# A fused sliding-window attention and two-layer MLP: weight loads in a row, a mask product on another engine, wider unused matmuls, and later steps placed anew

## The chip, the cores and the metric

The kernel runs on one core of a Trainium2 chip. The core has five engines that run their own instruction streams side by side: TensorE (PE in the profile, its weight loads PEld), VectorE (DVE), ScalarE (ACT), GpSimd (POOL) and SyncE (SP), which here only issues DMAs. The metric is device time in microseconds (us) of one execution.

## The reference

Input are q, k, v of shape (8 batches, 8 heads, 576 positions, 64), and two weight matrices, 512 x 2048 and 2048 x 512, all float32.

```
scores = (1/sqrt(64)) * q @ k^T                 # per batch and head, 576 x 576
scores = where(|i - j| <= 32, scores, -1e9)     # a band of 65 positions
attn   = exp(scores - max) / (sum + 1e-9)
x      = (attn @ v), heads side by side         # 4608 tokens x 512
h      = x @ w_in                               # 4608 x 2048
g      = max(0.01 * h, h)
out    = g @ w_out                              # 4608 x 512
```

## The kernel before

The schedule is written out by hand: what stands first in the program stands first on its engine, and each engine works strictly in that order.

**Attention.** The work is cut into steps i of a batch, a half of its 576 positions (288) and a pair of heads; i = 0 to 7 is batch 0 (first the four pairs of the first half), 8 to 15 batch 1. For each step `score(i)` (lines 411 to 439) multiplies the K blocks with Q on TensorE into one PSUM tile `ps`, ScalarE takes the exponential, and one engine multiplies the result with a 0/1 mask: VectorE where `masked_by=nc.vector` is given, GpSimd otherwise (line 436). `sums(i)` multiplies the masked result with a block matrix of ones on TensorE (`row_sums`, line 461) and takes the reciprocal on VectorE (`inverse`, line 469). `product(i)` multiplies it with V (line 484), and `scaled(i)` multiplies product and reciprocal on VectorE into `xT` (line 503). The PSUM tiles `x` (products) and `s` (row sums) have one buffer each; the row sums of steps 1 and 2 lie in the ring of four buffers `mm` that the MLP's first layer uses too. Masks are made on GpSimd and VectorE at the start.

**Loads of batches 0 and 1.** `load_qk(b, p)` (lines 68 to 97) issues one DMA for Q and one for K of a pair on SyncE. With `behind` given, a 1x1 memset on an engine (line 75) comes first, so that SyncE's issues start only when that engine has got there. `cast_qk` (line 280) casts what landed to bf16 on VectorE or GpSimd, and `transposes(b)` turns it on TensorE (line 322 for batch 0, 326 for batch 1), with copies on ScalarE. `load_cast_v` (line 147), `load_w_in` (line 687) and `load_w_out` (line 691) are DMAs that cast on the way; GpSimd issues them, so each stands in GpSimd's own order between its masks and casts. W_in comes in four loads of 512 columns, W_out in four loads of 512 rows.

**The MLP.** `h_first(0)` does the first four tiles (f = 0 to 3) of the first layer, column block by column block, as xT becomes ready; `h_tile(0, f)` does the other twelve, four matmuls of 288 columns each (line 527). Between them `second_half()` takes the next step of batch 0's second half: product, scaling, the row sums of the following step, and a score. After that come the first layer for the second half, `second_pair(p)` (transposes and casts of batch 1's pairs; the K casts of pairs 0 to 3 stand on GpSimd), and the second layer (lines 597 and 613). From then on a plan made at build time puts the attention of the other batches between the matmuls.

**Unused matmuls.** `warm_up(n, w)` (lines 622 to 628) issues n matmuls of 128 columns whose result nobody reads, at four places of the start: 28, 6, 8 and 4. The first 28 take a zeroed piece of the sixth `prob` buffer (`idle`, line 160), the others `ones_bd`.

Of the kernel before, what the change touches and what calls it, by code (L numbers as in the profile page):

```python
# [16 lines left out]
def kernel(  # L17
# [15 lines left out]
    nc = tc.nc  # L33
# [7 lines left out]
    NPAIR = H // 2  # L41
# [26 lines left out]
    def load_qk(b, p, behind=None):  # L68

        for into, src, name in ((qf, q, "qf"), (kf, k, "kf")):
            t = fload.tile([128, 2 * RUN * D], FP32, name=f"{name}{p}")
            if behind is not None:
                behind.memset(t[0:1, 0:1], 0.0)
                behind = None
            heads = src[b, 2 * p:2 * p + 2]
            if b == 0:

                into[b, p] = t[:, 0:NB * D]  # L80
                nc.sync.dma_start(
                    out=into[b, p], in_=heads.rearrange("a (p c) d -> (a p) (c d)", c=NB))
                continue
            t = t[0:96].rearrange("p (a r) -> p a r", a=2)
            if b < BY_DMA:
                nc.sync.dma_start(out=t, in_=heads.rearrange("a (p c) d -> p a (c d)", c=RUN))
            elif into is qf:
                nc.sync.dma_start(
                    out=t.rearrange("p a (g e) -> p a g e", g=3),
                    in_=heads.rearrange("a (g p c) d -> p a g (c d)", g=3, c=2),  # L90
                )
            else:
                nc.sync.dma_start(
                    out=t.rearrange("p a (c d) -> p a c d", d=D),
                    in_=heads.rearrange("a (c p) d -> p a c d", p=96),
                )
            into[b, p] = t
# [45 lines left out]
    def load_cast_v(b, p, heads=range(2)):  # L143

        for a in heads:
            r = slice(64 * a, 64 * a + 64)
            nc.gpsimd.dma_start(  # L147
                out=vbd[b % 2][r, p, :, r],
                in_=v[b, 2 * p + a].rearrange("(c p) d -> p c d", p=64),
            )  # L150

    NPROB = 6
    prob = const.tile([128, NPROB, 2, HALF], BF16)
# [3 lines left out]
    zero = const.tile([128, 1], BF16)  # L157
    nc.vector.memset(zero, 0.0)

    idle = prob[:, NPROB - 1, 0, 0:128]  # L160
    nc.vector.memset(idle, 0.0)
    for p in range(2):
        nc.vector.memset(vbd[0][:, p], 0.0)
# [3 lines left out]
    ones_bd = const.tile([128, 128], BF16)  # L167
# [18 lines left out]
    for lo in (0, 64):  # L186
        w = win[lo:lo + 64]
# [170 lines left out]
    def where(i):  # L358
        return i // 8, (i // 4) % 2, i % 4
# [6 lines left out]
    def score_blocks(i):  # L366
        p, bs = i % NPAIR, blocks_of(i)
        n = 2 * 64 * len(bs)
        lo = 512 * (i % 2)
        sc = ps[:, lo:lo + n].rearrange("p (a w c i) -> p a w c i", a=2, c=2, i=32)  # L370
        for w, (b, m) in enumerate(bs):
            tok = qz[b % 2][:, p, m // 3].rearrange("p a (c i) -> p a c i", c=2)
            at = 32 * (m % 3)
            nc.tensor.matmul(  # L374
                sc[:, :, w], kz[b % 2][:, p, 64 * m:64 * m + 128],
                tok[:, :, :, at:at + 32], start=True, stop=True,
            )
        e = attn.tile([128, 2 * HALF], BF16, name="e")
        nc.scalar.activation(out=e[:, 0:n], in_=ps[:, lo:lo + n], func=AF.Exp, scale=scale)  # L379
        pr = prob[:, i % NPROB].rearrange("p n i -> p (n i)")[:, 0:n]  # L380
        nc.gpsimd.tensor_mul(pr, e[:, 0:n], band.rearrange("p w c i -> p (w c i)")[:, 0:n])  # L381
        probs[i] = pr.rearrange("p (a w i) -> p a w i", a=2, i=64)
# [28 lines left out]
    def score(i, masked_by=nc.gpsimd):  # L411
        if i >= OLD:
            return score_blocks(i)
        b, hf, p = where(i)
        tok = qT[b][:, p, hf * HALF:hf * HALF + HALF]
        if b == 0:

            for a, n_, m in ((0, 0, 0), (1, 1, 0), (0, 0, 1), (1, 1, 1), (0, 0, 2),
                             (0, 1, 0), (1, 0, 0), (0, 1, 1), (1, 0, 1), (1, 0, 2)):
                blk, i0, n = WIN[hf][n_][m]  # L420
                r = slice(64 * a, 64 * a + 64)
                nc.tensor.matmul(
                    ps_v[r, n_, i0:i0 + n], first_keys[p][r, 64 * blk:64 * blk + 64],
                    tok[r, i0:i0 + n], start=True, stop=True,
                )
        else:
            for n_, blocks in enumerate(WIN[hf]):
                for blk, i0, n in blocks:
                    nc.tensor.matmul(
                        ps_v[:, n_, i0:i0 + n], kbd[b % 2][:, p, blk],  # L430
                        tok[:, i0:i0 + n], start=True, stop=True,
                    )
        e = attn.tile([128, 2 * HALF], BF16, name="e")
        nc.scalar.activation(out=e, in_=ps[:, P0:P0 + 2 * HALF], func=AF.Exp, scale=scale)  # L434
        pr = prob[:, i % NPROB]
        masked_by.tensor_mul(  # L436
            pr.rearrange("p n i -> p (n i)"), e, mask[hf].rearrange("p n i -> p (n i)"),
        )
        probs[i] = [pr, None, None]
# [9 lines left out]
    def row_sums(i):  # L449

        pr, both, _ = probs[i]
        if i in (1, 2):

            s = mmps.tile([128, 512], FP32, name="mm", tag="mm")[:, 0:HALF]
        else:
            s = xps.tile([128, 512], FP32, name="s")[:, 0:HALF]
        if both is not None:
            nc.tensor.matmul(s, ones_bd, both, start=True, stop=True)  # L458
        else:
            for n in range(2):  # L460
                nc.tensor.matmul(
                    s, ones_bd, pr[:, n],
                    start=(n == 0), stop=(n == 1),
                )
        probs[i][2] = s

    def inverse(i):
        r = recip.tile([128, HALF], FP32, name="r")
        nc.vector.reciprocal(r, probs[i][2])  # L469
        probs[i][2] = r  # L470

    def sums(i):
        if probs[i][2] is None:
            row_sums(i)
            inverse(i)
# [43 lines left out]
    while t0 < new:  # L519
        n = 256 if t0 < 2048 else min(512, new - t0)  # L520
# [52 lines left out]
    def h_first(g):  # L573

        hs = [mmps.tile([128, 512], FP32, name="mm", tag="mm") for _ in range(4)]
        yield hs[0]
        for c in range(DMC):
            for f in range(4):
                h_mms(g, f, hs[f], (c,))
            if c == DMC - 1:  # L580
                for f in range(4):
                    h_out(g, f, hs[f])
            yield
# [35 lines left out]
                nc.scalar.activation(out=o_sb, in_=o[j], func=AF.Copy)  # L619
                nc.sync.dma_start(out=out[ts(j, 128)], in_=o_sb)  # L620

    def warm_up(n, w=None):
        t = xps.tile([128, 512], FP32, name="x")
        w = ones_bd if w is None else w
        for _ in range(n):
            nc.tensor.matmul(
                t[:, 0:128], w, w, start=True, stop=True, skip_group_check=True,
            )

    def keep_busy(t, lo, n):  # L630
# [55 lines left out]
    def load_w_in(f0, f1):  # L686
        nc.gpsimd.dma_start(out=w_in_bf[:, :, f0:f1], in_=w_in_r[:, :, f0:f1])

    def load_w_out(i):
        c = slice(4 * i, 4 * i + 4)  # L690
        nc.gpsimd.dma_start(out=w_out_bf[:, c, :], in_=w_out_r[:, c, :])
# [3 lines left out]
    def clear_on_act(t):  # L695
        nc.scalar.activation(
            out=t.rearrange("p n j -> p (n j)"),
            in_=zero.to_broadcast([128, NB * 128]), func=AF.Copy,
        )

    warm_up(28, idle)
    clear_on_act(vbd[0][:, 3])
    clear_on_act(kbd[1][:, 0])
    cast_qk(0, 0, nc.vector, nc.vector)
# [5 lines left out]
    load_w_in(0, 512)  # L710
    next(first)
    next(first)
    warm_up(6)
    cast_qk(0, 1, nc.vector, nc.vector)
    score(0, masked_by=nc.vector)
    next(first)
# [4 lines left out]
    score(1, masked_by=nc.vector)  # L721
    next(first)
    next(first)
    warm_up(8)
    cast_qk(0, 3, nc.vector, nc.gpsimd)
    load_cast_v(0, 3, (1,))
    sums(1)
    score(2)
    load_w_in(512, 1024)
    next(first)  # L730
    next(first)
    warm_up(4)
    product(0)
    scaled(0)
    score(3)
    sums(2)
    load_w_in(1024, 1536)
    product(1)
    scaled(1)
    score(4)  # L740
    load_w_in(1536, 2048)
    h0 = h_first(0)
    h = next(h0)
    clear_on_act(kbd[1][:, 1])
# [7 lines left out]
    scaled(3)  # L752
    score(5)
    clear_on_act(kbd[1][:, 2])
    load_w_out(0)
    row_sums(4)
    inverse(4)
    next(h0)
    next(h0)
    for p in range(NPAIR):  # L760
        load_qk(1, p, nc.gpsimd if p == 0 else None)
    score(6)
    load_w_out(1)
    load_w_out(2)
# [3 lines left out]
    def second_half():  # L768

        i = state["done"]  # L770
        weighted(i)
        if i < 7:
            sums(i + 1)
        if i < 5:
            score(i + 3)
        state["done"] += 1

    for f in range(4, FFC):
        h_tile(0, f)
        if f in (4, 7, 11):  # L780
            second_half()
        if f == 4:
            load_w_out(3)
            for t in (vbd[1][:, 0], vbd[1][:, 1], kbd[1][:, 3]):
                nc.gpsimd.memset(t, 0.0)
# [48 lines left out]
    at, t = {1: 0.0}, 0.0  # L834
# [10 lines left out]
    t = at[2] - LEAD + 1.8  # L845
    while len(due) + 8 < NC:
# [3 lines left out]
        t = until  # L850
# [77 lines left out]
```

## Time and profile before

Three runs took 310.88, 310.92 and 311.04 us.

| | |
|---|---|
| median of the runs | 310.92 us |
| the profiled execution's own time | 311.2 us |
| its span, from the first to the last instruction | 309.5 us |
| TensorE busy | 298.5 us (96%) |
| VectorE, ScalarE, GpSimd busy | 224.2, 204.0, 200.7 us |
| HBM read and written | 36.70 and 9.44 MB |

In the profile an instruction's row has its line, engine, operation, the tiles it writes and reads by the program's names, and the shape; "x18" counts instructions put together. "[0.73 <-issue]" is idle time of the engine ahead of the row and what ended it, where "issue" means that the profile shows nothing that the engine waited for. PEq, POOLq and SPq are the sequencers of those engines, which issue DMAs. A DMA has its issue as a row and a time to landing. "q0" is the queue of the DMAs that GpSimd issues, "q1" SyncE's, and "instruction" queues bring the engines' programs.

### The profile page before, as it was taken

The numbers are of one execution on the slowest core, as the hardware profiler recorded it, in microseconds if no ns is written. First come the engines' busy times: TensorE is split into PE (matmuls) and PEld (weight loads), VectorE is DVE, ScalarE is ACT, GpSimd is POOL, SyncE is SP. The second block draws the span as 40 slices with busy tenths as digits, with TensorE's granted clock in tenths as the row PEclk, the third lists the DMA queues.
The fourth block names the chain that finished last, engine by engine and source line by source line (L and its number), as shares of the span: only waits on it lengthen the run. The fifth ranks groups of instructions, "written<-read, shape, count | busy, mean of one in ns | idle before, by whom it ended". The sixth has DMA issues, their size and how long they took to land.

```text
span 309.5 us, 6981 instructions
## 1 busy us (share of the span) xinstructions
PE 298.5 (96%) x2639; PEld 195.7 (63%) x2668; DVE 224.2 (72%) x302; ACT 204.0 (66%) x421; POOL 200.7 (65%) x254
## 2 busy tenths in 40 slices
PE   7789989999999999999999999999999999999996
PEld 6557855675846767685858585959555555444643
DVE  7899459797888987898799777898679866744000
ACT  7676864473956758585849584849589548842731
POOL 8889599969799997779579367578857522110000
PEclk9999999999999999999999999999999999999999
DMA  7999999996999799989999995995950110001002
GB/s 227 217 168 218 268 195 183 217 204 151 214 202 219 168 259 190 162 189 256 175 172 180 259 217 119 178 213 112 195 133 0 37 68 36 0 36 69 34 29 75
DMA packets 121506, 48.31 MB, mean 156 GB/s; under 512 B 96256, under 2 KB 115968, under 8 KB 121472
## 3 DMA queue, kind: packets, MB, share of 16 engines
q1 hardware_dynamic: 107776, 42.48, 68.0%
q0 software_dynamic: 13696, 5.38, 14.6%
q8 instruction: 21, 0.34, 0.5%
q14 instruction: 13, 0.11, 0.1%
HBM read 36.70 MB, written 9.44 MB: 149 GB/s over the span
## 4 chain that ended last, share of the span: by engine, by line
PE 74%; DMA 9%; POOL 9%; DVE 2%; SPq 2%; issue 2%; ACT 1%; POOLq 0%; ACTq 0%
PE mm L597 32%; PE mm L527 30%; DMA kf<-in_k_dram 6%; PE ps L374 3%; POOL prob L381 2%; PE mm L613 2%; DMA vbuf<-in_v_dram 2%; DVE r L469 2%; PE s L392 2%; PE x L392 2%; DMA set<-kb 1%; POOL kb L280 1%; SPq L112 1%; POOL set L147 1%; POOL qb L280 1%
## 5 line engine op out<-in xcount | busy, mean ns | idle before, releaser
L527 PE MATMUL mm<-xT,w_in_bf 128*128 128x256 bf16 (+3 forms) x956 | 133.1, 294 | 0.5 <-DVE r L469 0.3
L597 PE MATMUL mm<-w_out_bf,gT 128*128 128x512 bf16 (+2 forms) x537 | 122.5, 373 | 1.3
L401 DVE RECIPROCAL r<-r 128x256 f32<-128x256 f32 (+1 forms) x56 | 95.0, 1696 | 35.8 <-ACT r L400 35.3
L527 PEld LDWEIGHTS <-w_in_bf 128*128 128x128 bf16 x960 | 91.4, 98 | 30.1 <-DMA w_in_bf<-in_moe_w_in_dram 0.3
L381 POOL TENSOR_TENSOR prob<-e,band 128x512 bf16<-128x512 bf16 (+1 forms) x56 | 62.7, 1120 | 56.0 <-ACT e L379 54.6
L597 PEld LDWEIGHTS <-gT 128*128 128x128 bf16 x560 | 52.1, 98 | 54.1
L535 ACT ACTIVATE gT<-mm 128x288 bf16<-128x288 f32 (+2 forms) x112 | 50.0, 478 | 11.0 <-PE mm L527 8.2
L379 ACT ACTIVATE e<-ps 128x512 bf16<-128x512 f32 (+1 forms) x56 | 32.4, 579 | 28.0 <-PE ps L374 25.8
L602 ACT ACTIVATE o_sb<-mm 128x512 f32<-128x512 f32 (+2 forms) x35 | 20.5, 585 | 39.7 <-PE mm L597 39.4
L558 ACT ACTIVATE gT<-mm 128x512 bf16<-128x512 f32 x64 | 35.7, 596 | 5.5 <-PE mm L527 4.2
L469 DVE RECIPROCAL r<-s 128x288 f32<-128x288 f32 x14 | 27.3, 1950 | 1.5 <-PE s L458 0.9
L280 POOL CAST kb<-kf 96x768 bf16<-96x768 f32 (+1 forms) x30 | 24.9, 829 | 5.1 <-DMA kf<-in_k_dram 4.8
L405 DVE TENSOR_TENSOR xT<-x,r 64x256 bf16<-64x256 f32 (+1 forms) x56 | 24.4, 435 | 3.3
L405 DVE TENSOR_TENSOR xT<-s,r 64x256 bf16<-64x256 f32 (+1 forms) x56 | 24.3, 434 | 3.3
L306 DVE COPY set<-kT 64x576 bf16<-64x576 bf16 x48 | 21.4, 446 | 2.3 <-DMA kT<-qb 1.3
L374 PEld LDWEIGHTS <-set 128*128 128x128 bf16 x216 | 16.7, 98 | 9.8 <-DMA set<-kb 0.6
L374 PE MATMUL ps<-set 128*128 128x128 bf16 x216 | 21.4, 219 | 0.4 <-DMA set<-kb 0.4
L285 POOL CAST set<-vbuf 128x640 bf16<-128x640 f32 x24 | 17.2, 717 | 6.0 <-DMA vbuf<-in_v_dram 5.9
L280 POOL CAST qb<-qf 96x768 bf16<-96x768 f32 x24 | 19.7, 822 | 0.7 <-DMA qf<-in_q_dram 0.7
L436 POOL TENSOR_TENSOR prob<-e,mask 128x576 bf16<-128x576 bf16 x14 | 17.9, 1280 | 2.9 <-ACT e L434 2.9
L392 PEld LDWEIGHTS <-set 128*128 128x128 bf16 x432 | 18.0, 98 | 0.9 <-issue 0.4
L286 POOL CAST set<-vbuf 64x512 bf16<-64x512 f32 x24 | 14.7, 612 | 1.5
(96 smaller groups left out, 241.3 us busy)
## 6 DMA issues: line engine op xcount, KB each, us to landing
qf<-in_q_dram SPq DMA_DIRECT2D x32, 288.0 KB, 5.7
kf<-in_k_dram SPq DMA_DIRECT2D x32, 288.0 KB, 6.0
out_dram<-o_sb SPq DMA_DIRECT2D x35, 256.0 KB, 2.9
vbuf<-in_v_dram SPq DMA_DIRECT2D x15, 256.0 KB, 5.0
w_in_bf<-in_moe_w_in_dram POOLq DMA_DIRECT2D x4, 512.0 KB, 7.1
w_out_bf<-in_moe_w_out_dram POOLq DMA_DIRECT2D x4, 512.0 KB, 15.0
vbuf<-in_v_dram SPq DMA_DIRECT2D x10, 192.0 KB, 4.6
set<-in_v_dram POOLq DMA_DIRECT2D x16, 72.0 KB, 6.4
```

What stands on the lines that cost most here:

```text
L280: eng.tensor_copy(out=to, in_=tok)
L374: nc.tensor.matmul(sc[:, :, w], kz[b % 2][:, p, 64 * m:64 * m + 128], tok[:, :, :, at:at + 32], start=True, stop=True,)
L379: nc.scalar.activation(out=e[:, 0:n], in_=ps[:, lo:lo + n], func=AF.Exp, scale=scale)
L381: nc.gpsimd.tensor_mul(pr, e[:, 0:n], band.rearrange("p w c i -> p (w c i)")[:, 0:n])
L392: nc.tensor.matmul(x[:, a, w], vw[b % 2][:, p, m, a:a + 2].rearrange("p n d -> p (n d)"), pr[:, a, w], start=True, stop=True,)
L401: nc.vector.reciprocal(r[:, 0:n], r[:, 0:n])
L405: nc.vector.tensor_mul(xT[rows, p, t0:t0 + n].rearrange("p (w i c) -> p w c i", i=32, c=2), x[rows, a].rearrange("p (w c i) -> p w c i", c ...
L469: nc.vector.reciprocal(r, probs[i][2])
L527: nc.tensor.matmul(h[:, 0:n], w_in_bf[:, c, ts(f, 128)], xT[:, c, t0:t0 + n], start=(c == 0), stop=(c == DMC - 1),)
L535: nc.scalar.activation(out=to, in_=h, func=AF.Prelu, alpha=0.01)
L558: nc.scalar.activation(out=gT[:, f - 1:f + 1, t0:t0 + 256], in_=hh.rearrange("p (f t) -> p f t", f=2), func=AF.Prelu, alpha=0.01,)
L597: nc.tensor.matmul(o[:, lo:hi], gT[:, f, t0:t0 + 128], w_out_bf[:, f, lo:hi], start=(f == 0), stop=(f == FFC - 1),)
```

## The change

Five edits, all in the work up to the end of batch 0:

- The unused matmuls all read the zeroed piece, which is now 512 columns wide, and go up to 512 columns at a time: 7 of 512, 2 of 384, 2 of 512, 1 of 512 in place of 28, 6, 8 and 4 of 128.
- The loads of W_in's second, third and fourth part are issued in a row ahead of `score(2)`; before, each stood behind one of the scores 2, 3 and 4.
- The mask product of `score(2)` is on VectorE.
- The first W_out load stands behind `score(4)`, and the eight loads of batch 1 (with the 1x1 memset on GpSimd) directly behind `score(5)` and a clearing on ScalarE. Before, W_out's first part stood behind `score(5)`, and batch 1's loads behind it.
- The steps of batch 0's second half stand behind the first-layer tiles f = 5, 8, 11 instead of 4, 7, 11, and what goes with the first (the fourth W_out load and three memsets on GpSimd) moves with it.

```diff
-    idle = prob[:, NPROB - 1, 0, 0:128]
+    idle = prob[:, NPROB - 1].rearrange("p n i -> p (n i)")[:, 0:512]
     nc.vector.memset(idle, 0.0)
...
-    def warm_up(n, w=None):
+    def warm_up(n, w=512):
         t = xps.tile([128, 512], FP32, name="x")
-        w = ones_bd if w is None else w
         for _ in range(n):
             nc.tensor.matmul(
-                t[:, 0:128], w, w, start=True, stop=True, skip_group_check=True,
+                t[:, 0:w], idle[:, 0:128], idle[:, 0:w], start=True, stop=True,
+                skip_group_check=True,
             )
...
-    warm_up(28, idle)
+    warm_up(7)
...
-    warm_up(6)
+    warm_up(2, 384)
...
-    warm_up(8)
+    warm_up(2)
     cast_qk(0, 3, nc.vector, nc.gpsimd)
     load_cast_v(0, 3, (1,))
+    load_w_in(512, 1024)
+    load_w_in(1024, 1536)
+    load_w_in(1536, 2048)
     sums(1)
-    score(2)
-    load_w_in(512, 1024)
+    score(2, masked_by=nc.vector)
     next(first)
     next(first)
-    warm_up(4)
+    warm_up(1)
     product(0)
     scaled(0)
     score(3)
     sums(2)
-    load_w_in(1024, 1536)
     product(1)
     scaled(1)
     score(4)
-    load_w_in(1536, 2048)
+    load_w_out(0)
     h0 = h_first(0)
...
     score(5)
     clear_on_act(kbd[1][:, 2])
-    load_w_out(0)
+    for p in range(NPAIR):
+        load_qk(1, p, nc.gpsimd if p == 0 else None)
     row_sums(4)
     inverse(4)
     next(h0)
     next(h0)
-    for p in range(NPAIR):
-        load_qk(1, p, nc.gpsimd if p == 0 else None)
     score(6)
...
     for f in range(4, FFC):
         h_tile(0, f)
-        if f in (4, 7, 11):
+        if f in (5, 8, 11):
             second_half()
-        if f == 4:
+        if f == 5:
             load_w_out(3)
             for t in (vbd[1][:, 0], vbd[1][:, 1], kbd[1][:, 3]):
                 nc.gpsimd.memset(t, 0.0)
```

## The prediction

> **What bounds the kernel now.** I read the busy rows first (TensorE 298.5 of 309.5 us), then what TensorE waited for, then the order of time on TensorE, GpSimd and SyncE up to 45 us, because all edits lie there. The profiled execution took 311.2 us (span 309.5 and 1.7 around it), 0.28 us over the median of 310.92; the sum below is a difference, taken off the median.
>
> From the waits of TensorE:
>
> ```profile
> PE tp L326 <- POOL kb L280: 0.9, 1, 0.9
> PE x L626 <- issue: 0.7, 1, 0.7
> ...
> PE s L461 <- DVE r L469: 0.6, 1, 0.6
> ```
>
> Columns: total us, times, longest. After the start there are two places to win: an idle stretch of 0.9 us before batch 1's third K transpose, and a start-up in which TensorE waits for a reciprocal (0.6) and once for nothing shown ("issue", 0.7). From 41 us on the waits listed for TensorE add up to 0.7 us, so what moves there moves the end.
>
> TensorE in order of time, around both places (start, us, what; idle before and releaser in brackets):
>
> ```profile
> 12.91 0.34 PE L626 MATMUL x<-ones_bd 128*128 128x128 bf16 x3
> 13.98 0.22 PE L626 MATMUL x<-ones_bd 128*128 128x128 bf16 x1 [0.73 <-issue]
> 14.25 0.40 PE L484 MATMUL x<-prob,set 128*128 128x96 bf16 x5
> 14.58 0.43 PE L422 MATMUL ps<-set,kT 64*64 64x96 bf16 x10
> 14.94 0.42 PE L461 MATMUL mm<-prob,ones_bd 128*128 128x288 bf16 x2
> ...
> 39.42 0.42 PE L326 MATMUL tp<-ident,qb 96*128 96x96 bf16 x6
> 40.76 0.43 PE L326 MATMUL tp<-ident,kb 96*128 96x96 bf16 x6 [0.91 <-POOL kb L280]
> ```
>
> The fourth unused matmul of the third call stalls though it depends on nothing new; behind it stand product(0), score(3) and sums(2). GpSimd over the same time:
>
> ```profile
> 14.17 0.82 POOL L687 DMA_DIRECT2D w_in_bf<-in_moe_w_in_dram  x1
> ...
> 20.28 1.26 POOL L436 TENSOR_TENSOR prob<-e,mask 128x576 bf16<-128x576 bf16 x1 [0.40 <-ACT e L434]
> 21.50 0.81 POOL L691 DMA_DIRECT2D w_out_bf<-in_moe_w_out_dram  x1
> 22.30 0.09 POOL L75 MEMSET qf<- 1x1 f32 x1
> ...
> 36.08 0.82 POOL L280 CAST kb<-kf 96x768 bf16<-96x768 f32 x1 [2.31 <-DMA kf<-in_k_dram]
> 36.84 2.56 POOL L147 DMA_DIRECT2D set<-in_v_dram  x3
> 39.38 0.55 POOL L208 MEMSET band<- 128x512 bf16 x1
> 39.86 0.84 POOL L280 CAST kb<-kf 96x768 bf16<-96x768 f32 x1
> ```
>
> and the chain that ended last:
>
> ```profile
> 23.34 0.42 SPq L86
> 23.86 12.17 DMA kf<-in_k_dram
> 36.08 0.82 POOL kb L280
> ```
>
> The 1x1 memset at 22.30 releases SyncE's eight loads of batch 1. Its second K load is issued at 23.86 and lands at 36.03; only then come the cast, three V issues, a memset and the cast that TensorE waits for at 40.76. So TensorE resumes at (landing of that load) + 4.73 us, or at its own arrival (39.84), whichever is later.
>
> **The change part by part.**
>
> *Unused matmuls.* 28 of 128 columns become 7 of 512, then 6, 8, 4 become 2 of 384, 2 and 1 of 512: the same 3584, 768, 1024 and 512 columns. The first 28 take 3.17 us, 113 ns each; the later eight (0.62 us) 57 ns apart. No row shows 512 columns early on; 16 later ones take 3.45 us, 216 ns each, which at the slow start's rate (113 against 57) is about 0.43, so 7 x 0.43 = 3.0 us. Bounds: -0.2 to +0.2 us, before data that lands at its own time, so taken as nothing. The memset ahead grows from 64 to 256 words: between 0.11 us (64) and 0.54 (576), 0.27, so VectorE and TensorE start 0.16 us later. The second pair's casts wait for a DMA (VectorE idles 0.78 us before 6.72), which covers it; without that cover it would cost 0.16.
>
> *Instructions removed.* TensorE's program loses 34 matmuls and 34 weight loads (5338 to 5270). Counted in the program the stalled matmul is number 448; the instruction queue moves 16 KB packets (21, 0.34 MB), which at 5338 instructions is 254 each. One such packet runs between 11 and 12 us, while 1149 small V packets pass. I take the stall as a late packet of instructions. With 68 fewer ahead, number 448 is in the five scores before the keep-busy matmuls (at 15.8 before), over 2 us further on, and the packet is asked for some 1 us later: the stall should end before it is felt. Bounds: 0 (it moves along) to 0.73 us.
> [...]
>
> *Third mask.* On VectorE such a product takes 0.40 us (10.94), on GpSimd 1.27 (12.95 to 14.22). In VectorE's order it stands behind reciprocal(1) (12.09 + 1.94 = 14.03) and ends at 14.43, 0.21 later than now. VectorE has 0.66 us idle there, before scaled(0) at 14.69.
>
> *What both do to the chain.* Without the stall product(0) runs at 13.2; score(3) needs K's copy on ScalarE (13.30 + 0.66), so 14.0; sums(2) waits for the mask, 14.45 to 14.9; scaled(0) follows the mask, 14.43 to 14.89. Reciprocal(2) then starts at 14.93 instead of 15.39. The first-layer weights land at 16.45 (8.55 + 7.9) as before, and the fourth first-layer matmul waits for that reciprocal's buffer: 16.9 instead of 17.41. Reciprocal(3), row_sums(4) (19.98) and the rest follow: -0.46 us.
>
> *Second-half steps at f = 5, 8, 11.* One tile is 4 matmuls of 0.1225 us (16 take 1.96 from 27.95), 0.49 us. The step that starts sums(5) stands one tile later, which uses up the 0.46: reciprocal(5) starts at 23.04 as now. Between steps there are then 12, 12 matmuls (1.47 us) instead of 12, 16, while VectorE needs 1.95 + 0.46 us each: sums(6) waits to 25.06 (0.3 us), sums(7) to 27.5 (0.5). product(7), at 29.91 now, comes at 29.76. Of the 0.46 us, 0.15 are left. Its matmuls and sums, reciprocals and scalings all shift with it; the last mask product on GpSimd stays behind two W_out issues (25.85), and W_out(3) behind that, so neither moves by the tile.
>
> *Weights in a row, W_out(0) ahead.* Four weight issues of 0.81 us leave the gaps between masks. Three run from 12.53 to 14.97; mask(3) then waits only for its exponential (15.1 instead of 15.80) and mask(4) runs at 16.4. These loads are used from 23.4 on and the last lands at 26.5 (19.08 + 7.4), so their earlier landing gains TensorE nothing. W_out(0) is issued at 17.7, beside idle time.
>
> *Batch 1's loads.* mask(5) follows score(5), 0.46 earlier (19.8 to 21.05), and the memset follows directly instead of behind 0.81 us of issue: SyncE starts at 21.15 instead of 22.42, -1.27 us. Does the landing follow? SyncE's queue passes its first packets near 26.1, 3.6 us after the first issue; weights run at 0.20 MB per us until 24 and at 0.12 from 25, and from 28 both share. I take -1.2: landing at 34.8, so the third K cast is there at 34.8 + 4.73 = 39.55. Bounds: -1.4 (the weights' queue, with only 0.10 to 0.12 MB per us at 15 to 17, has no gap any more) to +2.0 (rival D). I take the near end because the sharing rows show the loads served beside a backlog of weights. The loads of batch 2, released by a memset on GpSimd at 46.40, and masks 8 and 9 shift with GpSimd.
>
> *Sum.* TensorE arrives at 39.84 - 0.15 = 39.69, after the cast (39.55): the 0.91 us go, TensorE resumes 40.76 - 39.69 = 1.07 us earlier. GpSimd, busy throughout from 36.84 to 60, shifts by 1.2, so it does not hold TensorE back; late next is the fourth K cast, 44.40 + 0.82 against a transpose at 45.27, which needs the same shift. I allow 0.07 for that: -1.0 us, 309.9.
>
> **The rivals.**
> B: the 0.73 stall stays on the path. Then the chain gains nothing, the later second-half steps cost 0.3 (sums(7) at 27.97), TensorE arrives at 40.14; the loads go only 0.82 earlier, the cast is there at 39.95. -0.6 us: 310.3. For it: the cause is inferred from a count.
> C: the K load lands when it did, since the DMA queues are full from 10 us on. The cast stays at 40.7, TensorE just waits longer: 310.9. Against it: the weights' gaps at 15 to 17 and 19 us.
> D, slower: W_out(0) is issued 3.5 us ahead of batch 1's loads instead of 0.9, and if they queue behind it whole, they start when its 0.52 MB have passed at 0.20 MB per us, near 28.0 instead of 26.1. The K load lands near 38.0, the cast at 42.8: +2.0 us, 312.9. It decides once the landing is later than 36.03. For it: the q queue's first packets came when the weight load issued at 19.08 was nearly done. Against it: W_out(0), landing at 32.6, did share with them.
> F: the second-half waits do not appear or the start gains more: TensorE arrives at 39.3, -1.5 us, 309.4.
>
> [...]
>
> **How the numbers follow.** A 0.50, F 0.07, B 0.17, C 0.14, D 0.12. Time of the likeliest: 309.9. 0.2% (0.62 us) is about what a measurement of this kernel tells from no change: faster means under 310.30. A, F and half of B give 0.65; the rest of B and most of C 0.20; D and what of C is worse 0.15. Range 309.2 to 311.1: it leaves out D and the far end of F, and holds A, B and C with their bounds.
>
> **What would show it.** Right: no "issue" idle near 13 us, product(0) near 13.3, reciprocal(2) near 14.9; SyncE's batch 1 loads at 21.1 to 21.3; the second K load landing at 34.6 to 35.0; the transpose of the third K at 39.7 with under 0.2 idle; waits of 0.3 to 0.5 at sums(6) and sums(7). Wrong if the "issue" idle only moves to another place on the chain, if the loads' time to landing grows by more than 0.3 from 12.2, or if GpSimd's later casts cannot follow, so that a wait at 45 or 87 us takes the gain back.

## The result, and the profile after

The changed kernel took 309.3 us (median of 6 runs, 308.53 to 310.32) against 310.98 for the kernel before (6 runs): a ratio of 0.9944, 95% interval 0.9920 to 0.9968. In two later comparisons the ratio was 0.9980 (0.9961 to 0.9999) and 0.9957 (0.9935 to 0.9979). Over all three, 30 runs of it average 309.52 us and the 69 runs of the kernel before beside them 310.69: 1.2 us, or 0.38%, where 1.0 us was forecast. Single runs of one kernel scatter by more than that (the kernel before from 309.03 to 312.58), so one trace shows one draw, and three traces of the changed kernel are read here.

The first has a span of 308.6 us, in an execution of 310.32. Waits of TensorE (total us, times, longest):

```profile
PE s L461 <- DVE r L469: 1.0, 2, 0.6
PE tp L322 <- POOL kb L280: 0.9, 1, 0.9
PE mm L527 <- DMA w_in_bf<-in_moe_w_in_dram: 0.8, 1, 0.8
...
PE mm L527 <- ACT gT L535: 0.5, 1, 0.5
```

The 0.9 us for batch 1's third K cast (line L326 before) and the "issue" wait are gone. New are a wait of 0.8 us for W_in and one of 0.5 put down to ScalarE. TensorE in order of time, first trace:

```profile
13.45 0.40 PE L484 MATMUL x<-prob,set 128*128 128x96 bf16 x5
...
24.80 0.66 PE L527 MATMUL mm<-xT,w_in_bf 128*128 128x288 bf16 x4 [0.45 <-ACT gT L535]
...
28.12 0.42 PE L461 MATMUL s<-prob,ones_bd 128*128 128x288 bf16 x2 [0.46 <-DVE r L469]
29.33 2.13 PE L527 MATMUL mm<-xT,w_in_bf 128*128 128x288 bf16 x16 [0.79 <-DMA w_in_bf<-in_moe_w_in_dram]
...
40.91 0.42 PE L326 MATMUL tp<-ident,kb 96*128 96x96 bf16 x6
```

product(0) runs at 13.45 without the stall. Tile 8 starts when W_in's third load lands (24.76), so the row at 24.80 is a wait for that DMA too; tile 12 waits for the fourth (29.28). In this execution W_in takes back all that was won: TensorE reaches the K transpose at 40.91, against 40.76 before, with nothing left to wait for. The 0.9 us by which this execution is still shorter than the profiled one before lie behind the K transpose, where two waits of the trace before (0.31 us at 87 us and 0.37 at 101) are missing. So this pair of traces does not show the forecast mechanism.

The second trace, of a faster execution (308.63 us, span 306.8):

```profile
13.12 0.40 PE L484 MATMUL x<-prob,set 128*128 128x96 bf16 x5
...
16.37 0.74 PE L527 MATMUL mm<-xT,w_in_bf 128*128 128x288 bf16 x4 [0.46 <-DMA w_in_bf<-in_moe_w_in_dram]
...
27.43 0.42 PE L461 MATMUL s<-prob,ones_bd 128*128 128x288 bf16 x2 [0.34 <-DVE r L469]
...
29.65 0.40 PE L484 MATMUL x<-prob,set 128*128 128x64 bf16 x5
...
39.25 0.42 PE L326 MATMUL tp<-ident,kb 96*128 96x96 bf16 x6
```

Here W_in is late only for the first tile (0.46) and the K transpose runs at 39.25, 1.51 us earlier than before. The third trace (309.23 us, span 307.4) lies between the two:

```profile
17.06 0.66 PE L527 MATMUL mm<-xT,w_in_bf 128*128 128x288 bf16 x4 [1.15 <-DMA w_in_bf<-in_moe_w_in_dram]
...
39.86 0.42 PE L326 MATMUL tp<-ident,kb 96*128 96x96 bf16 x6
```

Its first W_in load costs 1.15 us. The two waits at 87 and 101 us are in none of the three. From the 101st block-score matmul (line 374), at 161.12 us before, to the last matmul it is 145.28 us in every trace: what separates the kernels lies ahead of that point. More closely, from the third K transpose of batch 1 to the end of the span it is 267.5 to 267.9 us in ten of the fourteen traces, 268.5 to 268.8 in the three in which K lands latest (36.0 us or later; the table below), and 271.1 in one that is read in the last section.

The release of batch 1's loads in the second trace, SyncE's issues:

```profile
21.04 0.33 SPq L86 DMA_DIRECT2D qf<-in_q_dram  x1
...
22.45 0.41 SPq L86 DMA_DIRECT2D kf<-in_k_dram  x1
```

The first issue, 22.42 before, became 21.04; the second K load landed at 34.20 here, at 33.10 in the first trace and at 32.93 in the third, 36.02 before.

### The profile page after: what moved, and what is told of

The parts are those of the page before. It is cut to its first block, busy times and chain, and to the rows that moved or that the text cites. A ratio compares the mean times of both kernels' runs of the same rounds, so it can differ in the third digit from the quotient of the medians.

```text
span 308.6 us, 6941 instructions
## 1 busy us (share of the span) xinstructions
PE 299.1 (97%) x2634; PEld 192.6 (62%) x2634; DVE 223.6 (72%) x303; ACT 203.4 (66%) x421; POOL 199.0 (64%) x253
## 4 chain that ended last, share of the span: by engine, by line
PE 90%; DMA 5%; POOL 4%; issue 0%; ACT 0%; POOLq 0%; ACTq 0%
PE mm L527 39%; PE mm L597 38%; DMA w_in_bf<-in_moe_w_in_dram 5%; PE ps L374 4%; PE mm L613 2%; PE s L392 2%; PE x L392 2%; POOL set L147 2%; POOL w_in_bf L687 1%; PE x L484 1%; PE tp L326 1%; PE ps L429 1%; POOL kb L280 0%; POOL set L188 0%; POOL set L192 0%
## 5 line engine op out<-in xcount | busy, mean ns | idle before, releaser
L597 PE MATMUL mm<-w_out_bf,gT 128*128 128x512 bf16 (+2 forms) x560 | 124.6, 373 | 0.0
L401 DVE RECIPROCAL r<-r 128x256 f32<-128x256 f32 (+1 forms) x56 | 95.0, 1696 | 35.3 <-ACT r L400 34.9
L436 POOL TENSOR_TENSOR prob<-e,mask 128x576 bf16<-128x576 bf16 x13 | 16.7, 1287 | 7.1 <-ACT e L434 5.8
```

The costliest lines, as they stand in the source:

```text
L401: nc.vector.reciprocal(r[:, 0:n], r[:, 0:n])
L597: nc.tensor.matmul(o[:, lo:hi], gT[:, f, t0:t0 + 128], w_out_bf[:, f, lo:hi], start=(f == 0), stop=(f == FFC - 1),)
```

## The experiments

All compute the whole output. Each kernel was measured beside the kernel before in one of three series of runs (I to III), and the changed kernel again in II and III. "K1" is batch 1's second K load, with its issue on SyncE and its landing; "K transpose" is the start of the third K transpose of batch 1 on TensorE; these come from one trace of each row.

| kernel | series | K1 issued | K1 landed | K transpose | median us | ratio to before, 95% interval |
|---|---|---|---|---|---|---|
| before | I to III | 23.86 | 36.02 | 40.76 | 310.6 to 310.7 | |
| changed, first comparison | | 23.08 | 33.10 | 40.91 | 309.30 | 0.9944 (0.9920 to 0.9968) |
| changed, second | II | 22.45 | 34.20 | 39.25 | 309.72 | 0.9980 (0.9961 to 0.9999) |
| changed, third | III | 23.06 | 32.93 | 39.86 | 309.41 | 0.9957 (0.9935 to 0.9979) |
| wide unused matmuls alone | I | 24.11 | 35.91 | 40.61 | 310.78 | 1.0002 (0.9983 to 1.0020) |
| placement of the loads alone | I | 23.84 | 35.45 | 40.07 | 310.25 | 0.9994 (0.9973 to 1.0016) |
| W_in row and VectorE mask alone | II | 23.81 | 34.93 | 39.54 | 309.38 | 0.9969 (0.9947 to 0.9991) |
| row, mask and placement | II | 23.59 | 33.22 | 40.08 | 309.30 | 0.9958 (0.9939 to 0.9977) |
| the same again | III | 22.47 | 33.21 | 38.96 | 309.32 | 0.9951 (0.9933 to 0.9969) |
| changed, steps at 4, 7, 11 | I | 23.30 | 34.84 | 39.79 | 309.24 | 0.9954 (0.9934 to 0.9973) |
| changed, W_in spaced | I | 23.48 | 34.69 | 39.72 | 309.89 | 0.9984 (0.9963 to 1.0005) |
| the same again | II | 22.97 | 34.72 | 39.47 | 309.97 | 0.9988 (0.9966 to 1.0010) |
| row behind a GpSimd mask | III | 25.20 | 36.47 | 41.20 | 310.88 | 0.9997 (0.9976 to 1.0018) |
| before, batch 1's loads later | III | 27.89 | 39.66 | 44.52 | 313.32 | 1.0091 (1.0058 to 1.0125) |

**The unused matmuls alone.** The zeroed piece and `warm_up` are those of the change, and the counts:

```diff
-    warm_up(28, idle)
+    warm_up(7)
...
-    warm_up(6)
+    warm_up(2, 384)
...
-    warm_up(8)
+    warm_up(2)
...
-    warm_up(4)
+    warm_up(1)
```

> The kernel before with the unused matmuls alone changed (7 of 512 columns and so on). Theory 1 (the gain comes from the loads of batch 1 and from GpSimd running ahead; the start-up counts for little): the 0.73 us 'issue' idle near 13 us is gone and reciprocal(2) starts some 0.3 to 0.5 us earlier, but TensorE then waits for the third K cast of batch 1, which still comes near 40.7, so the end does not move: within 0.3 us of before, 310.9. Rival 2 (the gain is the start-up's 0.46 us): 310.4 to 310.5. Rival 3 (the idle is no packet of instructions): the idle stays at 13 us with its 0.7.

1.0002: no gain. Its trace has no "issue" wait, but reciprocal(2) starts at 15.43 (before: 15.39), because mask(1) took 1.00 us on VectorE instead of 0.40 (last section), and the wait for the K cast stays:

```profile
PE tp L326 <- POOL kb L280: 0.9, 1, 0.9
```

Wide unused matmuls by themselves are worth nothing that can be told. Neither of the two rivals is settled by it. The forecast earlier reciprocal(2) did not come, so the trace does not show what an earlier start-up would be worth (rival 2). And the stall is missing in this trace, but also in five of the seven traces of kernels that keep the narrow matmuls, so its absence cannot be put down to the wide ones (rival 3; more on it below).

**The placement of W_out(0) and of batch 1's loads alone.**

```diff
     load_w_in(1536, 2048)
+    load_w_out(0)
     h0 = h_first(0)
...
-    load_w_out(0)
+    for p in range(NPAIR):
+        load_qk(1, p, nc.gpsimd if p == 0 else None)
     row_sums(4)
```

> The kernel before with batch 1's loads behind score(5) and W_out(0) behind the fourth W_in load; W_in still behind scores 2, 3 and 4. Theory 1: the first load is issued at 21.6 instead of 22.4, the second K load lands 0.8 to 2.5 us earlier, the wait of 0.9 us near 40 goes, GpSimd runs ahead and the waits near 87 and 101 us (0.5 each) go too: 0.8 to 1.8 us faster than before, 309.1 to 310.1, unless W_in's last part lands later than TensorE needs it (29 us), which would take 0.3 to 0.8 of that back. Rival 2 (start-up): no change, 310.9.

0.9994: less than theory 1 said, though the interval reaches down to 0.8 us faster. The releasing memset came 0.57 us earlier and K1 landed 0.57 earlier (its own issue, the fourth of the eight, at 23.84 as before), and the K cast is waited for 0.5 us instead of 0.9:

```profile
PE tp L326 <- POOL kb L280: 0.5, 1, 0.5
```

An effect of 0.2 us cannot be told from none here. By itself this edit moves the release by less than the whole change does (0.57 us against 0.77 to 1.38), because mask(5) is no earlier.

**The changed kernel with the second-half steps back at 4, 7, 11.**

```diff
-        if f in (5, 8, 11):
+        if f in (4, 7, 11):
             second_half()
-        if f == 5:
+        if f == 4:
```

> The changed kernel with the second-half steps back behind tiles 4, 7, 11. By the prediction's step the later steps cost 0.3 us: 309.0 against 309.3. If W_in's landings (24.8 and 29.3 in the profile after) set the tiles f = 8 and f = 12, the waits for W_in only grow by what the reciprocals' wait loses and the time is that of the changed kernel, 309.1 to 309.5.

0.9954: near that of the changed kernel, which was not in this series. What the later steps cost cannot be told from nothing; the 0.3 us forecast for them are neither shown nor ruled out.

**The changed kernel with W_in's third and fourth load spaced again**, in two series.

```diff
-    load_w_in(1024, 1536)
-    load_w_in(1536, 2048)
...
     sums(2)
+    load_w_in(1024, 1536)
     product(1)
     scaled(1)
     score(4)
+    load_w_in(1536, 2048)
     load_w_out(0)
```

> The changed kernel with W_in's third and fourth load back behind the mask products of scores 3 and 4 (the second stays ahead of score 2). Theory 1 with late weights (loads in a row land later, up to 5.5 us behind the count of packets): W_in(2) and W_in(3) land by 24 and 27.5, the waits of 0.45 and 0.79 us for them go, 0.3 to 0.9 us faster than the changed kernel, 308.4 to 309.0. Rival 4 (the row of loads is where the gain comes from): slower than the changed kernel, 309.6 to 310.5.

> The changed kernel with W_in's third and fourth load behind the masks again, once more and beside the changed kernel. Theory 5: 0.3 to 0.7 us slower than the changed kernel of the same call, because mask(5) and the release of batch 1's loads wait behind two weight issues on GpSimd (21.7 against 21.1 us) and the weights' queue has gaps again. If the difference of 0.6 us seen between the two was scatter: within 0.2 us of it.

24 runs average 310.04 us, against 309.52 for 30 runs of the changed kernel: half a microsecond slower (standard error 0.23), where my theory of late weights wanted it faster. In series II, where both ran, the medians differ by 0.25 us and the averages by 0.47, so the forecast of 0.3 to 0.7 is neither clearly met nor missed. Having the third and fourth load in the row is then worth a little under half of the change's 1.2 us, with everything else in place. The traces do not show where: in both, K1 lands somewhat later than in the changed kernel (34.69, 34.72), but the K transpose, at 39.72 and 39.47, is within the changed kernel's 39.25 to 40.91. What makes it slower stays open.

**The row and the VectorE mask alone, and with the placement.** Theory 5, which the last forecast above names already: what decides is when batch 1's K lands, and the row sets that, because the weights ahead of it in the DMA queues are through sooner.

```diff
     load_cast_v(0, 3, (1,))
+    load_w_in(512, 1024)
+    load_w_in(1024, 1536)
+    load_w_in(1536, 2048)
     sums(1)
-    score(2)
-    load_w_in(512, 1024)
+    score(2, masked_by=nc.vector)
```

> The kernel before with the three W_in loads in a row and the third mask product on VectorE; W_out(0) and batch 1's loads stay where they were, and so do the unused matmuls and the second-half steps. Theory 5 (what decides is when batch 1's K lands, and the row empties the weights' queue sooner): the K load lands 0.4 to 1.0 us earlier than 36.0 and half of the change's gain is there, 309.9 to 310.4. Rival 2 (the start-up decides): the idle of 0.3 to 0.7 us at 13 us stays and the time is that of before, 310.6.

> The changed kernel with the narrow unused matmuls and with the second-half steps at 4, 7, 11: the W_in row, the mask on VectorE and the two placements of loads. Theory 5: row and placement together give the whole gain, 309.2 to 309.7, and the wait for the third K cast is under 0.2 us. Rival 6 (the wide unused matmuls are needed for it, through the start-up or through the clock that TensorE is granted near 10 us): at most half of the gain, 310.0 or more.

> The changed kernel once more, beside the three others on the same chip, for its spread and a second trace. If the lateness of W_in in the first trace (0.45 and 0.79 us at tiles 8 and 12) is a matter of one execution, this trace has less of it and TensorE reaches batch 1's third K transposes 0.5 to 1.2 us earlier than 40.9; if it belongs to the row of loads, W_in's last part lands after 28.5 again. Time 309.0 to 309.6.

The changed kernel's second trace has no lateness of W_in at tiles 8 and 12, so that belonged to one execution; its median, 309.72, is a little over the forecast. The row with the mask gives 0.9969 by itself, more than half of what the change gives and more than the forecast 309.9 to 310.4, although batch 1's loads are issued hardly earlier (22.29 against 22.42). The VectorE mask without the row was not tried. Transfers in the stretches ahead of them (from the start of each line: us, then busy times of PE, PEld, DVE, ACT and POOL; the last three figures are the clock, the DMA share and GB/s), before:

```profile
14.00:17.00 3.00, 2.75 (x38) 1.84 (x38) 2.09 (x3) 1.36 (x3) 2.20 (x3) 1.00 1.43 138
17.00:20.00 3.00, 2.09 (x29) 1.44 (x28) 2.69 (x4) 1.86 (x3) 2.86 (x4) 1.00 1.21 182
20.00:24.00 4.00, 3.91 (x46) 2.78 (x47) 3.80 (x5) 3.71 (x9) 3.04 (x4) 1.00 1.22 190
```

and with the row:

```profile
14.00:17.00 3.00, 2.45 (x37) 1.65 (x35) 2.86 (x4) 1.95 (x4) 2.57 (x4) 1.00 1.58 176
17.00:20.00 3.00, 2.13 (x28) 1.53 (x28) 2.69 (x4) 1.78 (x4) 1.18 (x1) 1.00 1.23 204
20.00:24.00 4.00, 3.91 (x47) 2.77 (x46) 3.80 (x5) 3.71 (x9) 3.13 (x4) 1.00 1.22 201
```

From 14 to 24 us that is 1.72 MB before (3 x 138 + 3 x 182 + 4 x 190 KB) and 1.94 with the row: 0.22 MB, which at 200 GB/s, about the rate of the last row, would be 1.1 us (an estimate). K1 lands 1.09 us earlier, and GpSimd's cast with it:

```profile
34.99 0.82 POOL L280 CAST kb<-kf 96x768 bf16<-96x768 f32 x1 [2.41 <-DMA kf<-in_k_dram]
...
38.67 0.82 POOL L280 CAST kb<-kf 96x768 bf16<-96x768 f32 x1 [0.16 <-DMA kf<-in_k_dram]
```

That the two agree so well is in part chance. In the seven traces with the row issued from 12 to 15 us, the same stretches move 1.86 to 2.00 MB, and K1 takes 9.6 to 11.8 us from issue to landing (10.7 on average). In the six with spaced loads they move 1.52 to 1.75 MB, and it takes 11.2 to 12.2 (11.7). The groups fit theory 5, but single traces do not line up: the changed kernel's second trace moves 1.90 MB and takes 11.75, that of the wide matmuls alone 1.56 and 11.80. So an earlier landing behind the row is seen; that the bytes ahead of it are the reason stays argued.

The placement on top takes K1 to 33.2, but TensorE then arrives later than the cast (in that trace at 40.08, behind a start-up that was itself slower), so its part, 0.11 points in the same series, is within the scatter. Over all comparisons, 23 runs of "row, mask and placement" average 309.29 (standard error 0.17), the changed kernel 309.52 (0.12). The two edits that "row, mask and placement" leaves out, the wide matmuls and the later steps, bring nothing that can be told.

**The row behind a GpSimd mask, and a dose.**

```diff
     score(2)
     load_w_in(512, 1024)
+    load_w_in(1024, 1536)
+    load_w_in(1536, 2048)
...
     sums(2)
-    load_w_in(1024, 1536)
...
     score(4)
-    load_w_in(1536, 2048)
```

> The kernel before with the three W_in loads in a row, but behind mask(2), which stays on GpSimd. Theory 5 (the row empties the weights' queue, whoever does the mask): the third and fourth load are issued 2 to 3 us earlier than before, batch 1's second K load lands at 35.0 to 35.5, TensorE resumes near 40.0 to 40.2 (mask(3) ends 0.8 us later and takes some 0.4 back): 309.8 to 310.2. If the mask on VectorE is what makes the row work: no faster than before, 310.5 or more.

0.9997. mask(2) ran at 14.03 on GpSimd in this trace (12.95 before; the granted clock was 0.50 from 10 to 12.5 us, so part of this delay is the execution's), the row was issued at 15.25 to 17.6 only, and mask(3) started at 17.57 instead of 15.80. K1 took 11.27 us from issue to landing, less than the 12.16 before, but it was issued 1.34 us later and landed at 36.47. Here the forecast of theory 5 failed: in a row is not enough, since three issues ahead of mask(3) hold up the masks and the release behind them. With mask(2) on VectorE the row is issued from 12.3 to 13.0 us and the release is not late. How row and mask share the gain was not separated further.

```diff
-    for p in range(NPAIR):
-        load_qk(1, p, nc.gpsimd if p == 0 else None)
     score(6)
     load_w_out(1)
     load_w_out(2)
+    for p in range(NPAIR):
+        load_qk(1, p, nc.gpsimd if p == 0 else None)
```

> The kernel before with batch 1's loads behind W_out's second and third load instead of ahead of them: the memset that releases them comes near 25.9 instead of 22.3, and nothing else changes. If the landing of batch 1's K sets the end (TensorE resumes 4.7 us after the second K load lands): it lands near 39.5, TensorE idles 3.5 to 4.5 us near 40 and the time is 313.0 to 314.5. If the loads are hidden and only a stretch of idle time moves: 310.6 to 311.2.

1.0091, 2.7 us slower, as the first forecast has it. TensorE, in order of time:

```profile
40.59 0.43 PE L326 MATMUL tp<-ident,kb 96*128 96x96 bf16 x6 [1.61 <-POOL kb L280]
...
44.52 0.43 PE L326 MATMUL tp<-ident,kb 96*128 96x96 bf16 x6 [1.05 <-POOL kb L280]
```

The memset came at 26.34, 4.04 us later than before; K1 landed at 39.66, 3.64 later, and the third K transpose started at 44.52, 3.76 later. All eight loads moved, and the K transposes of the first three pairs waited (1.32, 1.61 and 1.05 us). In the six traces in which the third K transpose follows its cast directly, the distance from K1's landing is 4.86, 4.74, 4.73, 4.70, 4.62 and 4.61 us. So these landings set the end until TensorE's own arrival takes over. In the trace of row and mask alone that is at K1 = 34.9; TensorE's arrival itself differs from trace to trace (38.96 to 40.91 where it waits for nothing).

> The changed kernel beside the three others of this call, as their measure: 309.3 to 309.7, as in the two calls before.

> The changed kernel without the wide unused matmuls and without the later second-half steps, again. If both edits are worth nothing or less: 0.1 to 0.5 us faster than the changed kernel of this call, about 309.2. If the 0.3 us between them in the call before was scatter: the same within 0.2 us.

309.41 and 309.32: no difference between the two that can be told.

## Why the prediction was right, and where it was not

*The bound.* Right: where TensorE waits for the third K cast, it resumes 4.6 to 4.9 us after batch 1's second K load lands (4.73 forecast), and the dose shows that the end follows.

*The sum.* 1.0 us forecast, 1.2 measured over three comparisons, 1.7 in the first. The first median, 309.3, is 0.6 us below the likeliest time of 309.9 and just inside the range (309.2), nearer to rival F's 309.4, which had a chance of 0.07. That the average agrees is in part luck: at the K transpose the three traces give 0.15 us later, 1.51 and 0.90 earlier, 0.75 on average, and two terms were off. "Batch 1's loads" forecast a release 1.27 us earlier and a landing at 34.8, with the time from issue to landing as before. The release came 1.26, 1.38 and 0.77 us earlier in the three traces, near the forecast. But K1 took 10.0, 11.75 and 9.9 us from issue to landing, against 12.16 before, and landed at 33.10, 34.20 and 32.93, beyond the bound of -1.4 each time. The row of loads was named only as a bound there ("no gap any more") and priced at nothing for TensorE; the row and mask alone moved K1 by 1.09 us and the time by 0.31%. And TensorE's arrival, forecast for 39.69, was 40.91, 39.25 and 39.86, so it, and no longer the K cast, sets the end, and the further landing gain is not used.

*The start-up.* The stall is in none of the traces with wide matmuls, as "Instructions removed" forecast. It is also in only two of the seven traces with narrow ones: 0.73 us in the trace before and 0.3 in that of the placement alone. So one profile made a matter of some executions look like a cost of the kernel. That it is a late packet of instructions rests on times, not on an experiment that moves the packet. In those seven traces the packet ends between 11.47 and 12.54 us, and matmul 448 starts 1.36 us or more after that. The two with the stall have the latest ends (12.54 with the matmul at 13.98, 12.36 with 13.71), and the distance there is 1.44 and 1.36 us. In the other five the packet ends by 11.96. This fits the packet as the cause, and does not show it. The prediction has the packet asked for some 1 us later in the changed kernel; that was my estimate, and the first trace does not show it: there the packet ran from 10.62 to 11.50 us, before from 11.60 to 12.54.

The chain came out as forecast in the second trace of the changed kernel: product(0) at 13.12 (13.2), reciprocal(2) at 14.82 (14.93), product(7) at 29.65 (29.76). But W_in's first load, which I had as a floor at 16.45 that did not bind, does bind once the chain is faster: 0.46 us at 16.37 there, and 1.15 us at 17.06 in the third trace. And the start won is easily lost again elsewhere, as to mask(1) in the first experiment and to W_in in the first trace above.

*The second-half steps.* The wait at sums(7) is there, 0.46, 0.34 and 0.34 us in the three traces (0.5 forecast); none is listed at sums(6) (0.3 forecast). Undoing the edit gained nothing that can be measured.

*Weights.* "Their earlier landing gains TensorE nothing" was right for TensorE's own use of them. Not foreseen was that they can land later: in the first trace the fourth load, issued 5 us earlier, landed at 29.28 instead of 26.45 and cost 0.79 us. In the second and third it landed at 25.43 and 25.68. Rival D's fear was that weights hold up batch 1's loads; what is seen in that trace is batch 1's loads, flowing from 24.7 on, beside a W_in that is not yet through.

*Rivals.* B (the stall stays) and D (K queues behind W_out) did not happen: with W_out(0) issued at 17.8, K1 landed at 33.10, ahead of W_out(0) itself (34.11). From 24 to 25 us, where batch 1's loads begin to flow in that trace, q0 passes 0.18 MB and q1 0.04. C (K lands when it did) did not happen either; with the placement alone K1 moved least, by 0.57 us.

*What the single profile hid.* The waits at 87 and 101 us of the trace before (0.31 and 0.37 us; the forecasts say 0.5 each) are missing in the trace of the unused matmuls alone, in which K lands nearly as late (35.91). So a kernel with that landing does not always have them. Later K landings can come with such a wait, too: 1.03 us at 102 us behind the GpSimd mask, 0.69 at 105 with the later loads.

## What to carry to other kernels

When a load that the end hangs on is issued late, beside other transfers (182 to 190 GB/s from 17 to 24 us before), look at its release and at what lies ahead of it: here a release 0.6 us earlier came with a landing 0.6 earlier (placement alone), and earlier transfers issued sooner, with hardly any change of the release, with one 1.1 earlier (row and mask). Once it lands before it is needed, the rest of the gain is not used: with K1 at 32.93 in the third trace the K transpose still ran at 39.86. An issue on GpSimd stands behind what comes before it in GpSimd's order: behind the mask product on GpSimd the row went out from 15.25 us on, with that product on VectorE from 12.3 to 13.0. So an operation that runs no sooner elsewhere can still pay: mask(2) ended at 14.45 on VectorE in the first trace of the changed kernel and at 14.22 on GpSimd before, and the row gave 0.9969 with the one and 0.9997 with the other. And where averages differ by 0.2 to 0.4% and single runs scatter by as much, one trace shows waits that the kernel does not always have: look for the same wait in traces of its neighbours before paying for its removal.

## What was not expected of the hardware

**Of a mask product on VectorE and a cast on GpSimd, one takes longer.** The second mask product (128x576 bf16, VectorE) and a cast on GpSimd start together in four traces. Before:

```profile
10.94 0.92 POOL L280 CAST kb<-kf 128x576 bf16<-128x576 f32 x1
10.94 0.40 DVE L436 TENSOR_TENSOR prob<-e,mask 128x576 bf16<-128x576 bf16 x1
```

and with the unused matmuls alone:

```profile
10.94 0.68 POOL L280 CAST kb<-kf 128x576 bf16<-128x576 f32 x1
10.94 1.00 DVE L436 TENSOR_TENSOR prob<-e,mask 128x576 bf16<-128x576 bf16 x1
```

One of the two stays short and the other takes longer: 0.40 and 0.92, or 1.00 and 0.68. In the other two traces it is 0.40 and 0.91 (row and mask alone) and 1.00 and 0.68 (W_in spaced, the first). Beside a reciprocal on VectorE the same cast took 0.66 (at 9.42 before). When VectorE's is the longer, the sums behind it start 0.6 us later (12.00 against 11.39). Why it is one or the other was not tested.

**TensorE's clock drops in the start-up of some executions.** In the trace with the placement alone the stretches from 7.5 to 12.5 us show a granted clock of 0.67 and 0.64:

```profile
7.50:10.00 2.50, 2.09 (x50) 1.39 (x52) 1.94 (x4) 1.46 (x3) 2.45 (x4) 0.67 1.46 301
10.00:12.50 2.50, 2.50 (x61) 2.18 (x56) 2.50 (x4) 1.73 (x3) 2.08 (x4) 0.64 2.18 168
```

Six of the fourteen traces have such stretches, with a mean granted clock of 0.994 or 0.995 over the execution; the other eight have 0.999 or 1.000. Of the 98 runs of the kernel before in the three series, the 48 with a mean clock of 0.999 or 1.000 average 310.32 us, the 31 near 0.994 average 310.79 and the 19 near 0.989 average 311.16. That is part of the scatter, and it was not in the prediction. Wide unused matmuls did not change how often it happens in a way that can be told: a full clock in 44 of 78 runs with them, in 78 of 162 without.

**One cast on VectorE took 5.43 us.** The second trace of "row, mask and placement" is of an execution of 311.79 us, where the median is 309.32. Its third K transpose runs at 38.96, the earliest of all, but the next transposes wait for VectorE's cast of the fourth pair's Q:

```profile
38.99 5.43 DVE L280 CAST qb<-qf 96x768 bf16<-96x768 f32 x1 [0.37 <-DMA qf<-in_q_dram]
44.48 0.43 PE L326 MATMUL tp<-ident,qb 96*128 96x96 bf16 x6 [1.17 <-DVE qb L280]
```

That Q load landed at 38.97, no later than in the changed kernel (38.58 to 39.54); the cast itself takes 0.56 to 1.57 us in the other thirteen traces. GpSimd ran V issues, two mask products and a cast in those 5.43 us. That would fit the longer times above, but nothing here tests it. A row sum behind GpSimd then waits too (1.25 us at 49.48), and from the K transpose to the end it is 271.1 us instead of 267.5 to 267.9. What decides this from run to run stays open.
